# A delta-rule layer feeding a cosine-gated FFN: the first pair's halved inverse widened to full columns in its copy

## The chip, the cores and the metric

The kernel runs on one core of one Trainium2 chip. The metric is the device time of one execution in microseconds (us), taken as the median of several runs. Engines are named as the profile names them: PE (TensorE, matrix products), DVE (VectorE), ACT (ScalarE), POOL (GpSimd) and SP (SyncE, which issues most transfers). "SPq" and "ACTq" are the instructions with which SP and ACT issue a transfer.

## The reference, cut to what matters

There are B = 4 batches, H = 8 heads, S = 768 positions and D = 48 features a head. The first part is a recurrence over the positions; the second is a feed-forward network with 384 inputs and 2048 hidden units, on the 3072 tokens that the recurrence gives.

```python
k_n = k / (norm(k, axis=-1) + 1e-6)
for t in range(S):
    y[:, :, t] = q_t @ state                              # per batch and head
    v_old = state.T @ k_t
    state = state + b_t * outer(k_t, v_t - v_old)
x = y.transpose(0, 2, 1, 3).reshape(B * S, H * D)         # (3072, 384)
h = x @ w_in
out = (h * cos(h)) @ w_out
```

## The kernel before

**Units and pairs.** The recurrence is computed in 24 units of C = 32 positions. Within a unit, the 32 steps are the solution of a lower triangular system, one 32x32 system for each of the 32 pairs of batch and head. Two units make a pair m; the 64 systems of a pair are inverted together, with half of the rows of each inverse in each half of the 128 partitions. The steps of a unit n are: its keys and queries are turned (`turn` on PE, `turn_out` to the tile kq_t on ACT), multiplied (`gram`), scaled and masked on DVE (`gram_keys` gives g, `gram_queries` gives tt), and g is stored to a DRAM scratch tile g_dr (`gram_put`). For a pair, `gram_get` loads g_dr as gb; `invert_eye` sets the inverse z to the identity; `invert` eliminates column after column (the lines 765 and 772); `put` stores z to the scratch tile z_dr; and `get` loads it for each unit in the layout that PE wants. Then `through_state`, `right_side`, `solve`, `solve_out`, `update` and `within` give the unit's outputs and the next state, and `features` and `features_out` turn the outputs into FFN inputs x_ffn.

**The first pair is halved.** All pairs but the first are inverted on POOL, in SBUF. The first pair (m = 0, `HALVED`, units 0 and 1) is inverted on DVE in a PSUM bank, and only as two 16x16 blocks on the diagonal of each system (`fold` brings the two blocks together; HC = 16). Half a of the partitions holds block a. The off-diagonal block g10 is kept in `off_blocks`. Such a unit is then solved in three steps: `solve_half` (p_w), `between` (p_v) and `solve` (p_u), with two copies between them (`half_out` on ACT, `between_out` on DVE, both into the tile u_half). `solve_half` and `solve` use the 32x32 block diagonal of the two inverted blocks, with zeros off the diagonal. In the kernel before this block diagonal lives in `half_zt`, two quarters of the tile halves_z, which is cleared once at the start. `invert_out` copies the 16 by 16 values of a partition from PSUM to SBUF, one `put` stores them, and `get` writes eight pieces a unit into the tile: four batches by two blocks. For unit 0 the four pieces of block 1 are issued by ACT and the others by SP.

**The weights.** w_in and w_out come as 64-bit integers' pairs of words and are put together on three engines, tile by tile: a load (`pairs`), two ACT instructions (532 and 534), two on DVE (538 and 543) and one on POOL (547). Twelve tiles belong to w_in and sixteen to w_out.

**The FFN.** For each pair of units there are hidden products (`hidden`, p_h), the gate h cos h (the lines 1005 to 1024), and output products (p_out). From the second or third pair on they are replaced by schemes with fewer products and more sums (`layer`, `strassen`).

**The order.** The order of all tasks on all engines is written by a list scheduler in Python, `Order`, when the program is built. Each task has an engine, an assumed cost, what it depends on, the buffers it makes and uses, and a due time. `NUDGE` shifts due times, `HOLD` keeps a task back until a time, and `ON_ACT` names the transfers that ACT issues in SP's place. The instructions then stand in that order on each engine and run in order. Every transfer from SP or ACT signals one of eight semaphores, taken in turn in the program's order; before it is issued, the transfer before it on the same semaphore must have landed.

**What sets the order at the start.** PE cannot be kept busy with FFN work until the first units have been through the recurrence and the first weights are there; afterwards the scheduler fills PE with FFN products between the steps of the units.

Of the kernel before, what the change touches and what calls it, by code (L numbers as in the profile page):

```python
# [11 lines left out]
FP = mybir.dt.float32  # L12
# [3 lines left out]
AF = mybir.ActivationFunctionType  # L16

C = 32
DP = 64
SPLIT = 2  # L20
# [25 lines left out]


class Order:
# [9 lines left out]
    WINDOW = 1261.351  # L58
# [14 lines left out]
    EARLY, NUDGE = 6, {('hidden', True): 61.2, ('out', False): 7.4, ('layer', False): 5.9, ('within', False): -4.5, ('hidden', 0, 8): 32.3, ('right', True): -39.1, ('inv', 0, 3): 5.0, ('solve_out', True): -66.4, ('turn', False): 28.3, ('rest', False): 22.3, ('rest', True): -14.8, ('state', False): -8.9, ('layer', True): 9.7, ('solve', True): 4.8, ('left', True): -6.1, ('left', False): 11.8, ('weigh', False): 11.0, ('cos', True): -11.4, ('inv', True): 4.0, ('update', False): -3.7, ('gate', False): 5.6}  # L73


    ON_ACT = {('weights', 9): 1, ('gram_put', 0): 1, ('weights', 14): 1, ('weights', 3): 1, ('gram_get', 1): 1, ('k', 7): 1, ('k', 4): 1, ('q', 3): 1, ('weights', 10): 1, ('gram_get', 2): 1, ('weights', 15): 1, ('weights', 5): 1, ('weights', 17): 1, ('weights', 6): 1, ('put', 0): 1, ('gram_get', 0): 1}
    HOLD = {('v', 5): 82.16, ('k', 8): 77.57, ('add', 9): 86.94, ('norms', 1, 1): 28.35, ('rest', 0, 2): 87.09, ('k', 6): 50.8, ('gate', 0, 4): 90.29, ('split', 11): 68.31, ('shift', 4): 40.04, ('eye', 1): 46.45, ('weights', 14): 75.83, ('features', 1): 93.82, ('split', 8): 56.33, ('split', 10): 65.61, ('get', 2): 96.99, ('half_out', 0): 53.13, ('split', 13): 77.98, ('shift', 5): 40.52, ('gram', 0): 16.72, ('norms', 2, 0): 49.12, ('add', 10): 91.37, ('add', 8): 66.01, ('right', 2): 94.14, ('q', 5): 52.19, ('add', 3): 36.15, ('square', 1, 0): 17.78, ('gram_queries', 2): 46.41, ('shift', 1): 23.89, ('shift', 16): 96.85, ('hidden', 0, 0): 70.69, ('gram_queries', 1): 23.15, ('split', 17): 99.7, ('add', 12): 77.47, ('get', 3): 101.36, ('weigh', 1): 61.19, ('v', 2): 42.92, ('eye', 2): 99.51, ('weights', 2): 18.93, ('gram_put', 2): 29.69, ('hidden', 0, 4): 80.59, ('turn_out', 1): 13.43, ('shift', 9): 60.15, ('weights', 1): 13.99, ('gram_keys', 3): 39.3, ('scale', 0, 0): 13.88, ('square', 3, 0): 65.52, ('turn', 0): 9.1, ('weigh', 0): 44.66, ('scale', 0, 1): 14.96}
# [19 lines left out]
    def add(  # L97
        self, key, engine, cost, emit, deps=(), makes=(), uses=(), moves=0.0, due=1e9
    ):

        assert key not in self.tasks, key
        if key in self.ON_ACT:
            assert moves
            engine = "ACT"
        self.tasks[key] = [engine, cost, due, emit, set(deps), makes, uses, moves]
        for t in uses:
            self.users[t] = self.users.get(t, 0) + 1
        for tag, t in makes:
            self.tiles[t] = tag
# [177 lines left out]
def kernel(  # L287
# [32 lines left out]
    nc = tc.nc  # L320
# [10 lines left out]
    ROWS = C // SPLIT  # L331
# [20 lines left out]
    def half(i):  # L352
        return slice(DP * i, DP * i + DP)
# [13 lines left out]
    def by_parity(t):  # L367
# [33 lines left out]
    def queue(*key):  # L401
        return nc.scalar if key in Order.ON_ACT else nc.sync

# [39 lines left out]
    near = 132 + C  # L443
# [5 lines left out]
    eye = consts[:, 132 + C : 132 + C + ROWS * C].rearrange("p (r i) -> p r i", i=C)  # L449
# [10 lines left out]
    for t in half_tiles:  # L460
        nc.vector.memset(t, 0.0)
        off_blocks.extend((t[:, 0], t[:, 1]))
        half_zt.extend((t[:, 2], t[:, 3]))
# [310 lines left out]
    def invert_out(m):  # L774
        z = work.tile([128, ROWS, C], FP, name="z", bufs=ZS)
        if m < HALVED:
            z = z.rearrange("p r i -> p (r i)")[:, 0 : HC * HC].rearrange(
                "p (r i) -> p r i", i=HC
            )
        nc.scalar.copy(z, zs[m])  # L780
        zs[m] = z

    def put(m):
        width = HC if m < HALVED else C
        z_drs[m] = dram.tile([ROWS, SPLIT, 2, H, B, width], FP, name="z_dr")
        queue("put", m).dma_start(
            out=z_drs[m].rearrange("r s u h b i -> (s u h b) r i"), in_=zs.pop(m)
        )

    def get(n):  # L790

        if n < 2 * HALVED:
            zts[n] = half_zt[n]
            for a in range(2):
                for b in range(B):
                    at = slice(C * b + HC * a, C * b + HC * a + HC)
                    (nc.scalar if a and n == 0 else queue("get", n)).dma_start(
                        out=zts[n][at, :, HC * a : HC * a + HC],
                        in_=z_drs[n // 2][:, a, n % 2, :, b].rearrange("r h i -> r h i"),
                    )  # L800
# [450 lines left out]
    def inverse(m):  # L1251
# [23 lines left out]
        if held:  # L1275
            add(("inv_out", m), "ACT", 0.65, lambda: invert_out(m), deps,
                makes=[("z", ("z", m))], uses=[z])
            deps = [("inv_out", m)]
        add(("put", m), "SP", 0.45, lambda: put(m), deps, makes=[("z_dr", ("z_dr", m))],
            uses=[("z", m)], moves=1.7)  # L1280

    def unit(n):
# [85 lines left out]
        if n < 2 * HALVED:  # L1368
# [11 lines left out]
                [("halves", m), ("u_half", n)] if n < 2 * HALVED else [("zt", n)]  # L1380
            ))
# [269 lines left out]
```

## Time and profile before

| | us |
|---|---|
| three runs | 670.53, 669.92, 669.42 (median 669.92) |
| the profiled execution, its own time | 669.99 |
| its span | 668.2 |
| PE busy in the span | 615.3 (92%) |
| DVE, POOL and ACT busy | 470.1, 348.5 and 246.2 |
| granted TensorE clock | 0.998 |
| packets of the transfers under 512 bytes | 207076 of 215645 |

The profile is of one execution. Its views give the busy time of each engine, the span in equal slices, the groups of instructions by line, and timelines with the time before which an engine was idle and what released it. A releaser is inferred from the semaphores; where a wait is for several of them, the view names the one that came last by its record. PE's instructions of one kind in a row are merged into one line of a timeline. Issue lines (SPq, ACTq) show the time that the issuing takes, not when the data land.

### The profile page before, as it was taken

To read this page: it belongs to the slowest core of one execution; us is meant where nothing else is said; L and a number is where in the kernel's file an instruction comes from. 1 tells how busy PE (TensorE), PEld (TensorE's weight loads), DVE (VectorE), ACT (ScalarE), POOL (GpSimd) and SP (SyncE) were. 2 spreads that over 40 slices of the span, in tenths; PEclk is the share of its full clock that TensorE was granted. 3 is DMA by queue.
4 is the path that set the end of the run, shared out by engine and by line. 5 is a ranking of instruction groups with operands and counts; after the bars stand their busy time and mean duration, and the time that the engine had idled before them with its cause. 6 is when DMAs were issued, how large, how long until landed. Compare 5 with 4: busy or idle time off the path is not lost.

```text
span 668.2 us, 27726 instructions
## 1 busy us (share of the span) xinstructions
PE 615.3 (92%) x12120; PEld 576.3 (86%) x12120; DVE 470.1 (70%) x892; ACT 246.2 (37%) x416; POOL 348.5 (52%) x734
## 2 busy tenths in 40 slices
PE   3316999999999999999999999999999999999997
PEld 3315878887989998999999999989999999989996
DVE  6695679788775875977866867767667656656661
ACT  3433545651243342433434334333324324323420
POOL 4458788978728628458438477158077067000000
PEclk9999999999999999999999999999999999999999
DMA  8866764574455244344434343342311311100000
GB/s 174 205 162 147 180 150 118 135 126 68 73 97 83 51 80 76 53 87 75 64 70 72 67 79 60 63 79 46 71 29 44 50 27 34 25 3 26 1 25 24
DMA packets 215645, 51.80 MB, mean 78 GB/s; under 512 B 207076, under 2 KB 210420, under 8 KB 215524
## 3 DMA queue, kind: packets, MB, share of 16 engines
q1 hardware_dynamic: 204516, 43.39, 34.4%
q10 hardware_dynamic: 10752, 6.20, 3.5%
q8 instruction: 95, 1.56, 1.0%
q0 software_dynamic: 256, 0.44, 0.3%
q14 instruction: 26, 0.21, 0.1%
HBM read 39.24 MB, written 10.75 MB: 75 GB/s over the span
## 4 chain that ended last, share of the span: by engine, by line
PE 82%; POOL 5%; DMA 5%; DVE 4%; issue 2%; ACT 1%; SPq 1%; ACTq 0%; DVEq 0%; POOLq 0%
PE p_h L1084 31%; PE p_out L1167 29%; PE p_kq L822 4%; PE p_h L965 3%; PE p_out L1110 3%; PE p_s L908 2%; PE p_u L885 2%; PE p_kq L925 2%; PE p_g L655 2%; POOL part L765 2%; POOL z L772 2%; PE p_o L1167 2%; PE p_z L944 1%; DMA g_dr<-g 1%; DMA qp<-in_q_dram 1%
## 5 line engine op out<-in xcount | busy, mean ns | idle before, releaser
L765 POOL TENSOR_TENSOR part<-z,gb 128x126 f32<-128x126 f32 (+22 forms) x341 | 135.8, 398 | 134.5 <-DMA gb<-g_dr 77.9
L772 POOL TENSOR_TENSOR z<-z,part 128x126 f32<-128x126 f32 (+22 forms) x341 | 138.5, 406 | 26.7
L1084 PE MATMUL p_h<-x_ffn,w_in 128*128 128x128 f32 x1120 | 145.5, 277 | 1.0 <-issue 1.0
L1084 PEld LDWEIGHTS p_h<-x_ffn,w_in 128*128 128x128 f32 x1120 | 135.5, 192 | 3.7 <-issue 2.1
L1167 PE MATMUL p_out<-w_out,g_ffn 128*128 128x192 f32 x672 | 122.9, 327 | 0.3 <-issue 0.3
L1005 ACT ACTIVATE turns<-p_h,quarter_turn 128x512 int32<-128x512 f32 x96 | 66.0, 687 | 150.3 <-DVE p_h L1103 106.9
L1167 PEld LDWEIGHTS p_out<-w_out,g_ffn 128*128 128x128 f32 x672 | 107.6, 190 | 1.0 <-issue 0.6
L1167 PE MATMUL p_out<-w_sum,g_ffn 128*128 128x192 f32 x496 | 91.3, 329 | 0.0
L1021 ACT ACTIVATE turns<-turns,halfpi 128x512 f32<-128x512 f32 x96 | 69.1, 721 | 42.3 <-DVE turns L1012 40.9
L1012 DVE SCALAR_TENSOR_TENSOR turns<-p_h,turns 128x512 f32<-128x512 f32 x96 | 65.6, 683 | 26.9 <-ACT turns L1005 26.8
L1167 PEld LDWEIGHTS p_out<-w_sum,g_ffn 128*128 128x128 f32 x496 | 79.4, 190 | 1.0
L1183 DVE TENSOR_TENSOR g_ffn<-g_ffn 128x512 f32<-128x512 f32 x88 | 61.9, 704 | 14.8 <-PE p_out L1167 13.9
L1100 ACT COPY g_ffn<-p_h 128x512 f32<-128x512 f32 x60 | 35.2, 586 | 96.4 <-PE p_h L1084 96.1
L1103 DVE TENSOR_TENSOR p_h<-g_ffn,p_h 128x512 f32<-128x512 f32 x60 | 41.7, 695 | 38.6 <-PE p_h L1084 37.8
L1024 DVE TENSOR_TENSOR g_ffn<-turns,p_h 128x512 f32<-128x512 f32 x96 | 64.9, 678 | 5.5 <-POOL w_out L547 3.3
L576 POOL TENSOR_TENSOR knrm<-ksum,halves 128x16 f32<-128x16 f32 (+1 forms) x14 | 37.3, 2665 | 39.8 <-DVE ksum L564 39.8
L965 PE MATMUL p_h<-x_ffn,w_in 128*128 128x128 f32 x384 | 47.7, 283 | 1.5 <-POOL w_in L547 1.3
L965 PEld LDWEIGHTS p_h<-x_ffn,w_in 128*128 128x128 f32 x384 | 45.3, 196 | 2.7 <-POOL w_in L547 1.7
L1217 DVE SCALAR_TENSOR_TENSOR o<-p_out,o 128x192 f32<-128x192 f32 x74 | 25.3, 354 | 29.5 <-PE p_out L1167 29.0
L1084 PE MATMUL p_h<-x_sum,in_sum 128*128 128x128 f32 x320 | 43.1, 278 | 0.7 <-issue 0.7
L1084 PEld LDWEIGHTS p_h<-x_sum,in_sum 128*128 128x128 f32 x320 | 40.2, 191 | 1.4 <-issue 0.8
L624 PE MATMUL p_t<-consts,kp 128*128 128x128 f32 x32 | 7.4, 373 | 31.8 <-DMA halves_z<-z_dr 19.4
(110 smaller groups left out, 780.4 us busy)
## 6 DMA issues: line engine op xcount, KB each, us to landing
pairs<-in_moe_w_out_dram SPq DMA_DIRECT2D x13, 384.0 KB
vp<-in_v_dram SPq DMA_DIRECT2D x96, 48.0 KB
gb<-g_dr SPq DMA_DIRECT2D x18, 256.0 KB
out_dram<-o SPq DMA_DIRECT2D x23, 192.0 KB
pairs<-in_moe_w_in_dram SPq DMA_DIRECT2D x7, 512.0 KB
kp<-in_k_dram SPq DMA_DIRECT2D x128, 24.0 KB
z_dr<-z SPq DMA_DIRECT2D x11, 256.0 KB
zt<-z_dr SPq DMA_DIRECT2D x88, 32.0 KB
```

The costliest lines, as they stand in the source:

```text
L576: nc.gpsimd.tensor_tensor(out=scales[m][2][:, part], in0=sums[m, part.start][:, 0:n], in1=halves[:, 0:n], op=ALU.pow,)
L765: eng.tensor_tensor(out=part, in0=z[:, 0:rows, j, None].to_broadcast(shape), in1=a[:, j, None, j + 1 :].to_broadcast(shape), op=ALU.mult,)
L772: eng.tensor_tensor(out=behind, in0=behind, in1=part, op=ALU.subtract)
L965: nc.tensor.matmul(p_h[:, i], w_in[:, t, (4 * k + i) * 128 : (4 * k + i + 1) * 128], xts[p][:, t, unit * 128 : (unit + 1) * 128], start=(t ...
L1005: nc.scalar.activation(turns[p, f], hidden_of(p, f), AF.Identity, bias=quarter_turn, scale=TURN)
L1012: nc.vector.scalar_tensor_tensor(out=r, in0=hidden_of(p, f), scalar=TURN, in1=t, op0=ALU.mult, op1=ALU.subtract,)
L1021: nc.scalar.activation(r, r, AF.Sin, bias=halfpi, scale=2.0 * math.pi)
L1024: nc.vector.tensor_tensor(out=place(p, f), in0=step_of(rests.pop((p, f)), f), in1=step_of(hidden_of(p, f), f), op=ALU.mult,)
L1084: nc.tensor.matmul(p_h[:, e], in_sum[:, odd_tile, 4 * s + e] if a == "s" else w_in[:, a, f * 128 : (f + 1) * 128], x_sums[p][:, unit] if b ...
L1103: nc.vector.tensor_tensor(out=block(p, s, 0, 1) if i == 3 else p_h, in0=block(p, s, *one), in1=p_h, op=ALU.add,)
L1167: nc.tensor.matmul(p_o, left(p, part, a)[:, e % 4], right(e, b), start=(e == 0), stop=(e == FT // 2 - 1), skip_group_check=True,)
L1183: nc.vector.tensor_tensor(out=left(p, s, to), in0=left(p, s, one), in1=left(p, s, two), op=op)
```

## The change

The copy `invert_out` of the first pair now writes full rows of 32 columns into z: it runs twice, once for each 16 columns, and multiplies by a mask of the partitions (`of_half`, a new constant of two columns), so that a partition of half a gets its 16 values in the columns of block a and zeros in the others. `put` stores z with two transfers, one for each half of the partitions. `get` is then the same as for all the other pairs: four transfers a unit, issued by SP, into a tile zt from a ring of two. `half_zt` is gone and halves_z has half its size. The load of weight tile 6 is no longer issued by ACT. The scheduler's costs of these tasks and its due times, nudges and holds are other values too, so some instructions stand in another order; the order on each engine is the same but for the places that the prediction speaks of and some neighbouring DVE and ACT instructions that change places.

```diff
@@ def _consts():
             p[:, None] // 16 % 2 == np.arange(2)[None, :],
+            p[:, None] // 64 == np.arange(2)[None, :],
             (row[:, :, None] == np.arange(C)).reshape(128, -1),
...
@@ class Order:
-    WINDOW = 1261.351
+    WINDOW = 1329.377
...
-    ON_ACT = {..., ('weights', 17): 1, ('weights', 6): 1, ('put', 0): 1, ('gram_get', 0): 1}
+    ON_ACT = {..., ('weights', 17): 1, ('put', 0): 1, ('gram_get', 0): 1}
...
-        if key[0] in ("k", "gram_put") and key[1] >= 8:
+        if key[0] in ("k", "gram_put") and key[1] >= 8 or key == ("put", 0):
             n //= 2
...
-    off_blocks, half_zt = [], []
+    off_blocks = []
...
-        ffn_pool.tile([128, 4, H, C], FP, name="halves_z", tag="g", bufs=GATES)
+        ffn_pool.tile([128, 2, H, C], FP, name="halves_z", tag="g", bufs=GATES)
...
+    of_half = consts[:, 132 + C : 134 + C]
...
     def invert_out(m):
         z = work.tile([128, ROWS, C], FP, name="z", bufs=ZS)
         if m < HALVED:
-            z = z.rearrange("p r i -> p (r i)")[:, 0 : HC * HC].rearrange(
-                "p (r i) -> p r i", i=HC
-            )
-        nc.scalar.copy(z, zs[m])
+            for a in range(2):
+                nc.scalar.activation(
+                    z[:, :, HC * a : HC * a + HC], zs[m], AF.Copy, scale=of_half[:, a : a + 1]
+                )
+        else:
+            nc.scalar.copy(z, zs[m])
         zs[m] = z

     def put(m):
-        width = HC if m < HALVED else C
-        z_drs[m] = dram.tile([ROWS, SPLIT, 2, H, B, width], FP, name="z_dr")
+        if m < HALVED:
+            z, z_drs[m] = zs.pop(m), dram.tile([2, HC, 2, H, B, C], FP, name="z_dr")
+            for a in range(2):
+                queue("put", m).dma_start(
+                    out=z_drs[m][a].rearrange("r u h b i -> (u h b) r i"), in_=z[half(a)]
+                )
+            return
+        z_drs[m] = dram.tile([ROWS, SPLIT, 2, H, B, C], FP, name="z_dr")
...
     def get(n):
+        zts[n] = work.tile([128, H, C], FP, name="zt")
         if n < 2 * HALVED:
-            zts[n] = half_zt[n]
-            for a in range(2):
-                for b in range(B):
-                    at = slice(C * b + HC * a, C * b + HC * a + HC)
-                    (nc.scalar if a and n == 0 else queue("get", n)).dma_start(
-                        out=zts[n][at, :, HC * a : HC * a + HC],
-                        in_=z_drs[n // 2][:, a, n % 2, :, b].rearrange("r h i -> r h i"),
-                    )
-            return
-        zts[n] = work.tile([128, H, C], FP, name="zt")
-        z_dr = z_drs[n // 2].rearrange("r s u h b i -> u b (r s) h i")[n % 2]
+            z_dr = z_drs[n // 2].rearrange("s r u h b i -> u b (s r) h i")[n % 2]
+        else:
+            z_dr = z_drs[n // 2].rearrange("r s u h b i -> u b (r s) h i")[n % 2]
         for b in range(B):
             queue("get", n).dma_start(out=zts[n][quarter(b)], in_=z_dr[b])
...
-    W_IN, W_OUT, LOADS = -17.551, -72.537, 365.19
+    W_IN, W_OUT, LOADS = -24.522, -78.511, 365.19
...
-    START = 47.26
+    START = 54.45
...
-            add(("inv_out", m), "ACT", 0.65, lambda: invert_out(m), deps,
+            add(("inv_out", m), "ACT", 0.75 if m < HALVED else 0.65, lambda: invert_out(m), deps,
...
-        add(("put", m), "SP", 0.45, lambda: put(m), deps, makes=[("z_dr", ("z_dr", m))],
+        add(("put", m), "SP", 0.98 if m < HALVED else 0.45, lambda: put(m), deps, makes=[("z_dr", ("z_dr", m))],
...
-        add(("get", n), "SP", 1.95 if n == 0 else 3.9 if n < 2 * HALVED else 1.9, lambda: get(n), [("put", m)],
-            makes=[] if n < 2 * HALVED else [("zt", ("zt", n))],
+        add(("get", n), "SP", 1.9, lambda: get(n), [("put", m)],
+            makes=[("zt", ("zt", n))],
```

More of the change, by code (lines that the diff above doesn't have):

```diff
@@ L71 @@
     CHANGE = 0.17
-    EARLY, NUDGE = 6, {('hidden', True): 61.2, ('out', False): 7.4, ('layer', False): 5.9, ('within', False): -4.5, ('hidden', 0, 8): 32.3, ('right', True): -39.1, ('inv', 0, 3): 5.0, ('solve_out', True): -66.4, ('turn', False): 28.3, ('rest', False): 22.3, ('rest', True): -14.8, ('state', False): -8.9, ('layer', True): 9.7, ('solve', True): 4.8, ('left', True): -6.1, ('left', False): 11.8, ('weigh', False): 11.0, ('cos', True): -11.4, ('inv', True): 4.0, ('update', False): -3.7, ('gate', False): 5.6}
@@ L76 @@
-    ON_ACT = {('weights', 9): 1, ('gram_put', 0): 1, ('weights', 14): 1, ('weights', 3): 1, ('gram_get', 1): 1, ('k', 7): 1, ('k', 4): 1, ('q', 3): 1, ('weights', 10): 1, ('gram_get', 2): 1, ('weights', 15): 1, ('weights', 5): 1, ('weights', 17): 1, ('weights', 6): 1, ('put', 0): 1, ('gram_get', 0): 1}
-    HOLD = {('v', 5): 82.16, ('k', 8): 77.57, ('add', 9): 86.94, ('norms', 1, 1): 28.35, ('rest', 0, 2): 87.09, ('k', 6): 50.8, ('gate', 0, 4): 90.29, ('split', 11): 68.31, ('shift', 4): 40.04, ('eye', 1): 46.45, ('weights', 14): 75.83, ('features', 1): 93.82, ('split', 8): 56.33, ('split', 10): 65.61, ('get', 2): 96.99, ('half_out', 0): 53.13, ('split', 13): 77.98, ('shift', 5): 40.52, ('gram', 0): 16.72, ('norms', 2, 0): 49.12, ('add', 10): 91.37, ('add', 8): 66.01, ('right', 2): 94.14, ('q', 5): 52.19, ('add', 3): 36.15, ('square', 1, 0): 17.78, ('gram_queries', 2): 46.41, ('shift', 1): 23.89, ('shift', 16): 96.85, ('hidden', 0, 0): 70.69, ('gram_queries', 1): 23.15, ('split', 17): 99.7, ('add', 12): 77.47, ('get', 3): 101.36, ('weigh', 1): 61.19, ('v', 2): 42.92, ('eye', 2): 99.51, ('weights', 2): 18.93, ('gram_put', 2): 29.69, ('hidden', 0, 4): 80.59, ('turn_out', 1): 13.43, ('shift', 9): 60.15, ('weights', 1): 13.99, ('gram_keys', 3): 39.3, ('scale', 0, 0): 13.88, ('square', 3, 0): 65.52, ('turn', 0): 9.1, ('weigh', 0): 44.66, ('scale', 0, 1): 14.96}
@@ new lines @@
+    EARLY, NUDGE = 6, {('hidden', True): 58.3, ('out', False): 7.4, ('layer', False): 5.9, ('within', False): -4.5, ('hidden', 0, 8): 32.3, ('solve_out', True): -64.9, ('turn', False): 32.4, ('rest', False): 22.3, ('state', False): -8.9, ('layer', True): 9.7, ('solve', True): 4.8, ('left', True): -9.9, ('left', False): 11.8, ('weigh', False): 11.0, ('inv', True): 4.0, ('update', False): -3.7, ('inv', 0, 1): 7.3}
+    ON_ACT = {('weights', 9): 1, ('gram_put', 0): 1, ('weights', 14): 1, ('weights', 3): 1, ('gram_get', 1): 1, ('k', 7): 1, ('k', 4): 1, ('q', 3): 1, ('weights', 10): 1, ('gram_get', 2): 1, ('weights', 15): 1, ('weights', 5): 1, ('weights', 17): 1, ('put', 0): 1, ('gram_get', 0): 1}
@@ new lines @@
+    HOLD = {('v', 5): 82.16, ('k', 8): 77.57, ('add', 9): 86.94, ('norms', 1, 1): 29.51, ('k', 6): 50.8, ('split', 11): 68.31, ('shift', 4): 40.04, ('weights', 14): 75.83, ('features', 1): 93.82, ('split', 8): 56.33, ('split', 10): 65.61, ('get', 2): 96.99, ('half_out', 0): 53.13, ('split', 13): 77.98, ('shift', 5): 40.52, ('gram', 0): 16.72, ('norms', 2, 0): 49.12, ('add', 10): 91.37, ('add', 8): 66.01, ('q', 5): 52.19, ('add', 3): 36.15, ('square', 1, 0): 17.78, ('gram_queries', 2): 46.41, ('shift', 1): 23.89, ('shift', 16): 96.85, ('hidden', 0, 0): 70.69, ('gram_queries', 1): 23.15, ('split', 17): 99.7, ('get', 3): 101.36, ('weigh', 1): 61.19, ('v', 2): 42.92, ('eye', 2): 99.51, ('gram_put', 2): 29.69, ('hidden', 0, 4): 80.59, ('shift', 9): 60.15, ('weights', 1): 13.99, ('gram_keys', 3): 39.3, ('scale', 0, 0): 13.88, ('square', 3, 0): 65.52, ('turn', 0): 9.1, ('weigh', 0): 44.66, ('scale', 0, 1): 14.96, ('turn', 1): 12.38}
@@ L442 @@
     consts = const.tile(list(consts_np.shape), FP, name="consts")
-    near = 132 + C
+    near = 134 + C
     nc.gpsimd.dma_start(out=consts[:, 0:near], in_=consts_dr.ap()[:, 0:near])
@@ L448 @@
     in_half = consts[:, 130 + C : 132 + C]
-    eye = consts[:, 132 + C : 132 + C + ROWS * C].rearrange("p (r i) -> p r i", i=C)
+    of_half = consts[:, 132 + C : 134 + C]
+    eye = consts[:, 134 + C : 134 + C + ROWS * C].rearrange("p (r i) -> p r i", i=C)
     for b in range(B):
@@ L462 @@
         off_blocks.extend((t[:, 0], t[:, 1]))
-        half_zt.extend((t[:, 2], t[:, 3]))
     halves = const.tile([128, 2, H], FP, name="halves")
@@ L1379, in unit @@
             makes=[("two", ("p_u", n))], uses=[("rhs", n) if n else ("vp", m)] + (
-                [("halves", m), ("u_half", n)] if n < 2 * HALVED else [("zt", n)]
-            ))
+                [("halves", m), ("u_half", n)] if n < 2 * HALVED else []
+            ) + [("zt", n)])
         add(("solve_out", n), "DVE", 1.12, lambda: solve_out(n), [("solve", n), scaled],
```

## The prediction

> **What bounds the kernel now.** I read the page's busy strips first, then the chain, then the time by stage, then the instructions of each engine between 40 and 92 us.
>
> ```profile
> span 668.2 us, 27726 instructions
> ...
> PE   3316999999999999999999999999999999999997
> ...
> PE 82%; POOL 5%; DMA 5%; DVE 4%; issue 2%; ACT 1%; SPq 1%; ACTq 0%; DVEq 0%; POOLq 0%
> ```
>
> Each digit of the strip is 16.7 us. TensorE (PE) is idle for most of the first four and full from the fifth on, and 82% of the chain that ended last is PE. So the time is set by when PE becomes full, and by the few holes after that. The stages (columns: stage, its length, busy time of PE, PEld, DVE, ACT, POOL):
>
> ```profile
> 49.30:60.00 10.70, 8.14 (x295) 7.06 (x295) 5.88 (x12) 3.07 (x6) 8.90 (x25) 1.00 0.74 193
> 60.00:67.40 7.40, 3.78 (x191) 3.06 (x189) 4.06 (x8) 2.54 (x5) 6.64 (x12) 1.00 0.54 110
> 67.40:80.00 12.60, 12.59 (x258) 12.11 (x259) 6.98 (x14) 6.40 (x12) 9.59 (x18) 1.00 0.74 184
> 80.00:100.00 20.00, 18.00 (x393) 15.39 (x392) 15.51 (x32) 9.61 (x19) 17.43 (x22) 1.00 0.66 150
> ```
>
> PE is idle 3.6 us in 60 to 67.4, nothing in 67.4 to 80, 2.0 us in 80 to 100. From 100 to 650 it is idle 4.9 us altogether. These are all the holes that an earlier transfer could close. What ends them is in the timelines (start, length, engine, instruction; in brackets the idle time before it and its releaser):
>
> ```profile
> 46.22 1.09 PE L624 MATMUL p_t<-consts,kp 128*128 128x128 f32 x4 [19.36 <-DMA halves_z<-z_dr]
> 49.32 1.81 PE L852 MATMUL p_w<-vp,halves_z 32*32 32x48 f32 x64 [1.16 <-ACT kq_t L634]
> 67.41 1.86 PE L852 MATMUL p_w<-rhs,halves_z 32*32 32x48 f32 x64 [1.32 <-ACT x_ffn L952]
> 91.47 2.72 PE L965 MATMUL p_h<-x_ffn,w_in 128*128 128x128 f32 x22 [1.06 <-POOL w_in L547]
> ...
> 48.68 0.59 ACT L634 COPY kq_t<-p_t 128x512 f32<-128x512 f32 x1
> 65.02 0.84 ACT L559 ACTIVATE ksq<-kp 128x768 f32<-128x768 f32 x1 [4.80 <-DMA qp<-in_q_dram]
> 66.87 0.47 ACT L952 COPY x_ffn<-p_z 128x384 f32<-128x384 f32 x1
> 73.06 0.56 ACT L532 ACTIVATE w_out<-pairs 128x384 f32<-128x384 f32 x1 [1.76 <-DMA pairs<-in_moe_w_out_dram]
> ...
> 45.21 2.45 SPq L797 DMA_DIRECT2D halves_z<-z_dr  x4
> 48.18 4.17 SPq L797 DMA_DIRECT2D halves_z<-z_dr  x8
> 69.13 0.52 SPq L524 DMA_DIRECT2D pairs<-in_moe_w_out_dram  x1
> ...
> 72.08 1.29 POOL L547 TENSOR_TENSOR w_in<-w_in,pairs 128x512 uint32<-128x512 uint32 x1 [1.29 <-DVE w_in L543]
> 78.99 1.01 POOL L547 TENSOR_TENSOR w_out<-w_out,pairs 128x384 uint32<-128x384 uint32 x1 [0.77 <-DVE w_out L543]
> ```
>
> What to see. The first solve (49.32) starts as kq_t's copy ends (48.68 + 0.59 = 49.27): it takes the PSUM bank that turn(4) held. Turn(4) at 46.22 is put down to a transfer of halves_z, which it does not read; in the built program it waits for the DVE's tt(2), which ended at 46.12. The last get of unit 0 on SP ended its issue at 47.66, so the transfer and the copy come due together, and the copy decides. The second solve (67.41) waits for x_ffn's copy, which sat on ACT behind ksq and a split (65.02 to 66.9), and ksq had waited 4.8 us for the last loads of k and q. Those loads stood on SP behind the gets: 2.45 + 4.17 us of issue. The hole at 91.47 waits for POOL, which has worked almost without a gap since 43.7.
>
> **What the skill says.** The Trainium skill, DMA: Bandwidth & Descriptors, Issuing engines are not separate DMA queues: issuing from several engines saves only issue time. Here that issue time is the point: 12 gets cost SP 6.6 us. The same page, Rules for kernel authors, advises against two transfers for two halves of the partitions, since both run over the same engines; the trace of before shows no such pair for the put. VectorE: DVE Perf Modes, The TRN2 errata, gives a ScalarE copy from PSUM as 172 cycles plus one an element at 1.2 GHz: 357 ns for 256 elements, and the trace has 0.37 us for that copy (L780). SBUF — State Buffer, its introduction: a DVE and a POOL instruction can lock each other out of a shared port; agreed, the shift L543 takes 0.42 us alone and 1.50 us beside POOL's adds.
>
> **The change part by part.**
>
> *ACT before the put.* One copy (0.37 us) becomes two of the same size: +0.37 us (between the skill's 0.36 and the 0.62 of a 128x512 copy, should a strided write cost like a full tile; I take 0.37, the row of the same size). One put becomes two issues of 0.38 and a gap of 0.1: +0.45. The put's second half leaves 0.8 us later, 38.6 for 37.8. Behind it on ACT stand a split, ksq and the loads of gb(1), which left at 41.57 after a wait for a g_dr store; ACT had over 1 us to spare there. Four gets leave ACT (2.05 us), which had nothing urgent after them. Cost on the path: 0. The cover is that wait and, for the split, DVE, which takes its result only at 41.5.
>
> *Packets.* 2048 for the put and 1024 a unit for the gets, as before, at 128 bytes for 64. The data is 0.13 MB more each way, in a stretch that moves 300 GB/s: 0.4 us each at most.
>
> *Order on SP.* Every hardware transfer takes one of eight semaphores in turn, and waits for the landing of the one eight earlier. The order of the built program shows what this does. (w0 to w11 are the tiles of w_in, w12 to w27 those of w_out, in the order of loading.) The load of w6 moves from ACT (30.66) to SP (after v at 32.3); it needs 4 us and is used at 38.2, so it costs 0. The load of w7, issued at 38.83 before, must now wait for the first half of the put. The other pairs' full put of 2048 packets took 4.4 us (88.35 to the get at 92.7), so half lands after some 3 us, at 41.2; w7 leaves 2.4 us later. Unit 0's second get waits for w7 (4.4 us, as w11 took from 65.27 to the split at 69.70, so 45.6), the fourth for gb(1) (45.2 before). Gets at 43.9, 45.6, 46.1 and 46.6, the last issued by 47.0 and landed 1.8 later, as k's last load was (63.2 to 65.0): 48.8. The copy at 49.27 still decides. First solve: 0, between 0 and +1 us.
>
> *Further on SP.* The load w8 leaves at 47.1 (47.77), unit 1's four gets at 47.1 to 49.1 in place of 48.18 to 52.35, v to 52. Then q's first transfer waits for the load of w10, issued by ACT at 53.06 and landed by 56.9, when ACT's next transfer on its semaphore went out; so of the 3 us only part survives. Then q, and k for unit 6 at 58.8 to 61 (60.04 to 63.2). SP is 2.2 us ahead; ksq runs at 62.8 and ACT is free when p_z ends at 66.09. x_ffn's copy 0.47, the wait for it 0.07: second solve at 66.65, **0.75 us earlier**. rhs(1) on DVE no longer stands behind the sum either (66.76 before) and is done by 65.9.
>
> *ACT and POOL after that.* The order puts the first w_out split (w12) ahead of u_half(1) on ACT, and w12's add ahead of w11's on POOL. w12 leaves SP at 66.6 in place of 69.13, lands 3.9 later at 70.5, is split by 71.6; u_half is done by 72.1. PE needs it at 66.65 + 1.79 + 4.19 = 72.6: half a microsecond to spare. POOL comes to w12's add at 70.8 and waits for the DVE shift until 72.5 (1.7 for 1.29 us), then has 1.0 + 1.3 us of adds, 3.9 of inverse and 1.0 for w13, whose load is also earlier, so the 0.77 at 78.99 goes: 79.7 for 80.0. If w12 lands 0.7 earlier it is 79.0. So the weights that PE waits for at 91.47 (w9 and w10, behind that inverse on POOL) come 0.3 to 1.0 us earlier. PE arrives 0.75 earlier, so this hole decides: gain **0.3 to 1.0**, and I take 0.7.
>
> *The rest.* halves_z is cleared over 512 columns in place of 1024 (0.91 us before, at 3.9 us, with DVE idle afterwards) and the constants grow by two columns: 0. Unit 0's scale moves within the inverse on DVE, same sum: 0. At two places, one about 205 us, PE, DVE and ACT stand in another order. PE has the same instructions there, and no other engine releases it after 150 us in before: I take 0, and 0.8 either way, out of the 3.8 us of holes from 150 to 650.
>
> Sum: 669.99 (the profiled execution; span 668.2 and 1.8 around it) − 0.7 = 669.3. The median of three runs is 669.92, so 669.2.
>
> **The rivals.**
> *More is won.* If POOL loses both waits, at 72 and 79 (2.06 us), it is ahead by more than PE is, PE's two waits for it near 90 (0.21 + 1.06) close, and the gain is 0.75 + 1.27, with the 0.34 at 111 at most 2.4: 667.5 to 668.5. For it: from 57 us on SP's lead may grow, as four transfers fewer hold its semaphores. Against: w12's add stands ahead of w11's.
> *SP's lead is eaten and the time stays.* The waits for the put, w7 and w10 replace the issue time. ksq then still runs at 65, and PE keeps 67.4: 669.9, within 0.5.
> *Slower: u_half(1) waits behind w12's split.* ACT is in order. If SP is not ahead when it issues w12, the split starts at 73.06 as before, u_half ends at 74.6 and PE, which ran p_v at 73.39, does so 1.2 us later: 671.1. If w7's detour also delays the first solve by 1 us: 672.1. It decides from a landing of w12 after 71.9 on (71.9 + 1.0 + 0.47 = 73.4), microsecond for microsecond. For it: the lead is 2.5 us, made of landings I bounded and did not see. Against: in before SP had idle stretches of 3.3 us at 42 that shrink.
> *The change does not do what it says:* the masks write zeros into the columns that the old tile held as zeros, so solve reads the same values; no more work for PE.
>
> **Numbers.** The forecast (0.3 to 1.0 gained, so 668.9 to 669.6, with the late order 668.1 to 670.4) has a chance of 0.42, the larger gain 0.24, no gain 0.12, the slower case 0.22. A measurement tells about 0.2% here, 1.34 us: 668.6 and 671.3. The forecast gives 0.12 to faster, 0.28 to the same and 0.02 to slower; the larger gain 0.22 and 0.02; the third case is the same; the slower one gives 0.02 to the same. In all 0.34 faster, 0.44 same, 0.22 slower. The range is 667.4 to 671.5: it leaves out the far half of the slower case and the best of the larger gain.
>
> **What would show it.** Right: first solve at 49.3, second at 66.7, ksq by 63, the w12 load issued near 66.6, PE's last wait for POOL at 90.5 to 91.2. Wrong: w7 landing after 46, a first solve that waits for zt, p_v of unit 1 released by u_half, or a PE stage after 100 us with over 1 us more idle than now.

## The result, and the profile after

The changed kernel is slower. Beside the kernel before it took 673.82 us (median of 9 runs) against 671.06 us (9 runs): ratio **1.0042**, 95% interval 1.0026 to 1.0059. A second comparison (after_2 below) gave 1.0067 (1.0041 to 1.0092, 6 runs). The prediction said 669.2 us, range 667.4 to 671.5, and it gave the slower side 0.22. The rival that it called "u_half(1) waits behind w12's split" is what happened; it priced it at 671.1 to 672.1.

One execution of either kernel differs from the next by several us: the runs of the kernel before lie between 667.6 and 677.6. Part of it arises at the start: the fourth run of p_g matmuls on PE (the products of unit 3, ahead of the long first wait) began between 25.5 and 30.0 us in the profiled executions below. Another part arises after PE's last hole for POOL (91 to 99 us), as is shown further down. So times of two profiles are compared here with care: what happened to the whole is read from the medians, and "rest" in the tables is the profiled time less the start of that fourth p_g (before: 669.99 − 25.68 = 644.3; after: 674.50 − 25.52 = 649.0).

The page of the changed kernel, its span, two strips and its chain by engine:

```profile
span 672.7 us, 27716 instructions
...
PE   3316889999999999999999999999999999999997
...
PEclk9999699999999999999999999999999999999999
...
PE 78%; DMA 7%; SPq 4%; POOL 4%; issue 3%; DVE 2%; ACT 1%; ACTq 0%; DVEq 0%; POOLq 0%
```

PE is full from the seventh slice on, where it was full from the fifth: the fifth and sixth slices (67 to 101 us) have 8 for 9. On the chain that ended last, DMA has 7% for 5% and SP's issuing (SPq) 4% for 1%: the added time is upstream of PE. The same four stages as before (stage, length, busy time of PE, PEld, DVE, ACT, POOL, granted TensorE clock, DMA share, GB/s):

```profile
49.30:60.00 10.70, 7.36 (x268) 6.46 (x272) 5.11 (x11) 3.12 (x6) 8.91 (x24) 1.00 0.77 200
60.00:67.40 7.40, 3.75 (x226) 3.13 (x219) 3.42 (x6) 0.95 (x2) 6.69 (x12) 0.82 0.43 73
67.40:80.00 12.60, 9.26 (x162) 8.52 (x161) 5.61 (x10) 5.22 (x11) 5.21 (x9) 0.64 0.77 198
80.00:100.00 20.00, 18.08 (x443) 15.74 (x442) 15.66 (x25) 9.56 (x18) 18.13 (x29) 0.96 0.48 105
```

The loss is in the third: PE is busy 9.26 us of 12.6, where it was busy all 12.59 before, and POOL 5.21 where it had 9.59. Two engines stand still at once. Who holds them is in the timelines of PE, ACT and POOL (start, length, engine, instruction; in brackets the idle time before it and its releaser):

```profile
49.68 1.72 PE L854 MATMUL p_w<-vp,zt 32*32 32x48 f32 x64 [1.16 <-ACT kq_t L635]
...
69.32 1.50 PE L854 MATMUL p_w<-rhs,zt 32*32 32x48 f32 x64 [1.46 <-ACT x_ffn L954]
...
77.58 0.88 PE L854 MATMUL p_v<-u_half,halves_z 32*32 32x48 f32 x64 [1.88 <-ACT u_half L864]
...
96.95 2.72 PE L967 MATMUL p_h<-x_ffn,w_in 128*128 128x128 f32 x22 [1.06 <-POOL w_in L548]
```

```profile
54.24 0.66 ACT L533 ACTIVATE w_in<-pairs 128x512 f32<-128x512 f32 x1 [2.27 <-DMA pairs<-in_moe_w_in_dram]
54.30 0.35 ACTq L525 DMA_DIRECT2D pairs<-in_moe_w_in_dram  x1
...
66.93 0.84 ACT L560 ACTIVATE ksq<-kp 128x768 f32<-128x768 f32 x1 [5.76 <-DMA qp<-in_q_dram]
...
76.19 0.54 ACT L533 ACTIVATE w_out<-pairs 128x384 f32<-128x384 f32 x1 [2.65 <-DMA pairs<-in_moe_w_out_dram]
...
77.06 0.46 ACT L864 COPY u_half<-p_w 128x384 f32<-128x384 f32 x1
```

```profile
78.10 1.01 POOL L548 TENSOR_TENSOR w_out<-w_out,pairs 128x384 uint32<-128x384 uint32 x1 [6.92 <-DVE w_out L544]
```

The first solve is where it was (49.68 for 49.32). The second is 1.9 us later, since ksq starts 1.9 later. Then both late orders bite: w12 is split at 76.19, u_half(1) is copied behind it at 77.06, and p_v, which found its input ready at 73.39 before, waits 1.88 us and starts at 77.58; POOL, with w12's add ahead of w11's, waits 6.92 us, where it waited 1.29 for w11. PE's hole for POOL comes at 96.95 for 91.47.

SP's own timeline and its waits between 38 and 75 us (instruction, what it waited for: total us, times, longest) tell why w12 is late:

```profile
41.66 0.35 SPq L525 DMA_DIRECT2D pairs<-in_moe_w_in_dram  x1
...
59.13 3.06 SPq L420 DMA_DIRECT2D qp<-in_q_dram  x4
62.63 2.53 SPq L420 DMA_DIRECT2D kp<-in_k_dram  x4
...
71.61 1.78 SPq L525 DMA_DIRECT2D pairs<-in_moe_w_out_dram  x1
```

```profile
SPq L420 <- DMA pairs<-in_moe_w_in_dram: 6.0, 2, 3.2
SPq L708 <- DVE g L667: 3.3, 1, 3.3
SPq L525 <- DMA z_dr<-z: 2.5, 1, 2.5
```

SP stood 6.0 us, in two waits, ahead of transfers of q and v until the load of a weight tile had landed; the kernel before has no such wait there. In the built program the two are a transfer of v behind w8 and the first transfer of q behind w10, each sharing a semaphore with it. The 2.5 us are w7's load behind the first half of the put, as predicted.

### The profile page after: what moved, and what is told of

Read it like the earlier page. It is cut to its first block, busy times and chain, and to the rows that moved or that the text cites. A ratio compares the mean times of both kernels' runs of the same rounds, so it can differ in the third digit from the quotient of the medians.

```text
span 672.7 us, 27716 instructions
## 1 busy us (share of the span) xinstructions
PE 616.3 (92%) x12120; PEld 578.1 (86%) x12120; DVE 468.3 (70%) x892; ACT 246.0 (37%) x417; POOL 347.2 (52%) x734
## 4 chain that ended last, share of the span: by engine, by line
PE 78%; DMA 7%; SPq 4%; POOL 4%; issue 3%; DVE 2%; ACT 1%; ACTq 0%; DVEq 0%; POOLq 0%
PE p_h L1086 28%; PE p_out L1169 27%; PE p_h L967 4%; PE p_kq L824 4%; SPq L420 3%; PE p_out L1112 3%; PE p_s L910 2%; PE p_u L887 2%; PE p_kq L927 2%; PE p_g L656 2%; DMA pairs<-in_moe_w_in_dram 2%; PE p_o L1169 2%; SPq L431 2%; POOL part L766 1%; POOL z L773 1%
## 5 line engine op out<-in xcount | busy, mean ns | idle before, releaser
L766 POOL TENSOR_TENSOR part<-z,gb 128x126 f32<-128x126 f32 (+22 forms) x341 | 133.1, 390 | 133.0 <-DMA gb<-g_dr 98.8
L773 POOL TENSOR_TENSOR z<-z,part 128x126 f32<-128x126 f32 (+22 forms) x341 | 140.4, 412 | 26.7
L1086 PEld LDWEIGHTS p_h<-x_ffn,w_in 128*128 128x128 f32 x1120 | 135.4, 192 | 1.5
L967 PEld LDWEIGHTS p_h<-x_ffn,w_in 128*128 128x128 f32 x384 | 47.6, 205 | 2.9 <-POOL w_in L548 1.3
L1219 DVE SCALAR_TENSOR_TENSOR o<-p_out,o 128x192 f32<-128x192 f32 x74 | 25.3, 354 | 28.2 <-PE p_out L1169 27.5
```

Of the source, the lines that this page charges most:

```text
L766: eng.tensor_tensor(out=part, in0=z[:, 0:rows, j, None].to_broadcast(shape), in1=a[:, j, None, j + 1 :].to_broadcast(shape), op=ALU.mult,)
L773: eng.tensor_tensor(out=behind, in0=behind, in1=part, op=ALU.subtract)
L967: nc.tensor.matmul(p_h[:, i], w_in[:, t, (4 * k + i) * 128 : (4 * k + i + 1) * 128], xts[p][:, t, unit * 128 : (unit + 1) * 128], start=(t ...
L1086: nc.tensor.matmul(p_h[:, e], in_sum[:, odd_tile, 4 * s + e] if a == "s" else w_in[:, a, f * 128 : (f + 1) * 128], x_sums[p][:, unit] if b ...
```

## The experiments

A kernel that is said to move a task has the scheduler's plan unchanged; after planning, the named task is moved in the list by which the instructions are written, and nothing else. Such a kernel has six more lines ahead of the copied ones, so L854 of the changed kernel is L860 there. The rivals are: **T1**, the loss is the order of instructions and the semaphores that go with it; **R1**, the loss is the new form itself; **R3**, a lower TensorE clock or a slower fetch of instructions. Ratios are to the kernel before in the same comparison, with their 95% interval.

### Form and order apart

form_alone is the kernel before with the new `invert_out`, `put`, `get`, constant and tiles:

```diff
-    halves_z 4 quarters; one narrow put; get: 8 pieces a unit into half_zt
+    halves_z 2 quarters; two copies with of_half; two puts; get: 4 pieces a unit into zt
     WINDOW, NUDGE, HOLD, ON_ACT, START and the costs: as before
```

> The order of before on every engine, with the new form of the first pair's inverse alone: two copies of the inverse, two puts, four gets a unit. Theory T1 (the loss comes from the new order, and from which transfer has to wait for which because of the eight semaphores, not from the form): the load of w7 waits only for a transfer of v here and leaves near 38.8 us; the second solve starts at 66.7 to 67.5, p_v of unit 1 by 73.5, and the time is that of the kernel before within 1 us (ratio 0.998 to 1.001). Rival R1 (the form costs it: 128-byte packets, two puts, a later copy): most of the 2.8 us is here, ratio 1.003 to 1.005, second solve at 68.5 or later. Rival R3 (a lower TensorE clock or slower instruction fetch in this program): no prediction for the second solve; the stretch from 67 to 80 us would show a clock well under 1.

order_alone is the reverse, the changed kernel's order with the old form:

```diff
     WINDOW, NUDGE, HOLD, ON_ACT, START and the costs: as in the changed kernel
-    two copies with of_half; two puts; get: 4 pieces a unit into zt
+    one copy, one narrow put; get: 8 pieces a unit into half_zt
```

> The form of before (one narrow put, twelve gets) in the new order: the load of w6 on SP, v ahead of q, u_half(1) behind w12's split on ACT, w12's add ahead of w11's on POOL. T1: SP has no lead here, so w12 lands near 72.5 as before, u_half(1) ends near 74.6, p_v of unit 1 starts near 74.6 (before 73.39) and POOL waits 2 to 4 us for w12; ratio 1.002 to 1.005. R1: same as before within 0.1%. If the loss needs both the form and the order (w7 held by the put, which only the two together give), this one shows 1.2 us at most, ratio 1.000 to 1.002.

| kernel | median us (runs) | ratio to before | profiled us | fourth p_g at | rest |
|---|---|---|---|---|---|
| form_alone | 672.30 (22) | 1.0000 (0.9985 to 1.0016) | 672.52 | 28.20 | 644.3 |
| order_alone | 674.59 (22) | 1.0043 (1.0026 to 1.0060) | 676.24 | 27.30 | 648.9 |

The form costs nothing that can be measured (by its interval 0.0016 at most), and the order alone costs as much as the whole change. That is R1 refuted. In PE's timeline of form_alone p_v finds its input ready although the second solve is at 68.38; in order_alone, with the old form, it waits:

```profile
73.49 0.88 PE L854 MATMUL p_v<-u_half,halves_z 32*32 32x48 f32 x64
```

```profile
78.28 0.88 PE L852 MATMUL p_v<-u_half,halves_z 32*32 32x48 f32 x64 [2.43 <-ACT u_half L862]
```

Three details of the expectations were off. The second solve of form_alone was late by 0.9 us against its range, and that cost nothing. In order_alone w12 did not land near 72.5: its split started at 76.89. And there the first solve waited 2.17 us for halves_z, up to 54.08, as SP's gets of unit 0 left at 47.86 (45.21 in before).

**R3**: the clock falls with the same two kernels. Here is the stretch from 67 to 75 us of the changed kernel and of order_alone (columns as above):

```profile
67.00:75.00 8.00, 6.54 (x89) 6.05 (x88) 3.62 (x6) 3.46 (x6) 3.63 (x8) 0.50 0.67 151
```

```profile
67.00:75.00 8.00, 6.56 (x142) 5.95 (x143) 3.50 (x6) 3.56 (x6) 6.01 (x12) 1.00 0.77 181
```

The granted clock is 0.50 in one and 1.00 in the other, with equal loss. form_alone, too, had 0.50 from 65 to 67 us and 0.72 from 67 to 75, without a loss. Instruction fetch had no experiment of its own. What speaks against it: the waits of PE ahead of the second solve that no semaphore explains ("issue", before p_g and p_kq) were 3.66 us in after and 3.69 in a_w12 below, which loses nothing.

### Undoing the late order in the changed kernel

```diff
+    MOVES = [(("half_out", 1), "before", ("split", 12)),   # u_half(1) on ACT: a_act, a_uhalf
+             (("add", 12), "before", ("add", 13))]         # w12's add on POOL: a_pool, a_uhalf
```

Both moves (a_uhalf):

> The changed kernel with two instructions put back in their old places: u_half(1) ahead of w12's split on ACT, and w12's add behind the sixth step of the inverse on POOL. T1: nothing changes until the second solve (69.3), p_v of unit 1 then starts at 75.3 to 75.6 (77.58 in the changed kernel), POOL's 6.9 us wait is under 2, and 1.5 to 2.5 us of the loss come back: ratio 0.999 to 1.001 of before. If the late second solve alone sets the time (T1's other half), only 0.5 us come back, ratio 1.003. R1 and R3: no change, ratio 1.004.

The first alone (a_act):

> The changed kernel with only the ACT half of the earlier repair: u_half(1) goes ahead of w12's split, w12's add stays ahead of w11's on POOL. T2 (both places must be repaired, as PE's hole near 91 to 97 us waits for POOL, and POOL waits 5 to 7 us for w12): p_v of unit 1 no longer waits, but PE then waits 2 to 3 us for POOL at the hole and nothing is gained: ratio to before 1.003 to 1.0045. Rival (PE's wait for u_half is the loss, POOL's is hidden): the ratio falls to 0.998 to 1.001, as with both repairs.

The second alone (a_pool):

> The other half: w12's add goes behind the sixth step of the inverse on POOL, u_half(1) stays behind w12's split on ACT. T2: POOL's wait falls under 2.5 us and its hole no longer decides, so the time is set by PE's own lateness: p_v of unit 1 still waits about 2 us for u_half, of which the 1.1 us hole for POOL takes back half: ratio 1.001 to 1.003. Rival (POOL's wait alone is the loss): 0.998 to 1.001. Rival (u_half alone is the loss): 1.004.

| kernel | median us (22 runs each) | ratio to before | profiled us | fourth p_g at | rest |
|---|---|---|---|---|---|
| a_uhalf | 671.17 | 0.9985 (0.9969 to 1.0000) | 671.60 | 27.03 | 644.6 |
| a_act | 673.49 | 1.0016 (1.0001 to 1.0032) | 673.48 | 28.16 | 645.3 |
| a_pool | 673.31 | 1.0017 (0.9997 to 1.0038) | 675.99 | 29.00 | 647.0 |

Both moves together take back all of the loss, each alone more than half by its median. The expectation for a_act (nothing, since PE would then wait for POOL) was wrong, as was its rival (all). In the traces the two waits are indeed separate. PE's p_v in a_uhalf, and POOL's wait there, now again for w11:

```profile
75.73 0.88 PE L860 MATMUL p_v<-u_half,halves_z 32*32 32x48 f32 x64
```

```profile
74.42 1.29 POOL L554 TENSOR_TENSOR w_in<-w_in,pairs 128x512 uint32<-128x512 uint32 x1 [2.18 <-DVE w_in L550]
```

In a_act POOL still waits 5.21 us (its timeline), in a_pool PE still waits 2.23 (PE's timeline):

```profile
78.07 1.01 POOL L554 TENSOR_TENSOR w_out<-w_out,pairs 128x384 uint32<-128x384 uint32 x1 [5.21 <-DVE w_out L550]
```

```profile
78.04 1.50 PE L860 MATMUL p_v<-u_half,halves_z 32*32 32x48 f32 x64 [2.23 <-ACT u_half L870]
```

### Putting the late order into the kernel before

```diff
+    MOVES = [(("half_out", 1), "after", ("split", 12)),    # b_act, b_late
+             (("add", 12), "before", ("add", 11))]         # b_pool, b_late
```

> The kernel before with only the late order of the changed one: u_half(1) behind w12's split on ACT, w12's add ahead of w11's on POOL; the early part, its transfers and the form stay as they were. T1: w12 is split at 73.06 to 74 as before, u_half(1) ends near 74.5, p_v of unit 1 starts 1.2 us later, POOL waits 3 us more for w12; ratio 1.002 to 1.005. Rival (the late order costs only because w7, w8 and w10 come late in the changed kernel): 1.000 to 1.001.

> The kernel before with only u_half(1) moved behind w12's split on ACT. As the prediction priced it: p_v of unit 1 starts 1.2 us later, and PE's hole for POOL takes some of it back: ratio 1.000 to 1.002. Rival (ACT's half is the mis-sized one): 1.004 or more, with PE waiting over 2 us for u_half.

> The kernel before with only w12's add moved ahead of w11's on POOL. If the price that was left out is POOL's: POOL, which has set PE's last hole in every trace so far, waits 4 to 6 us for w12 in place of 1.3 for w11, less the 1.0 us add and the 0.8 us wait that it no longer has later; ratio 1.003 to 1.005. Rival (POOL's wait is hidden and only both together cost): under 1.001.

| kernel | median us (runs) | ratio to before | profiled us | fourth p_g at | rest |
|---|---|---|---|---|---|
| b_late | 674.95 (6) | 1.0058 (1.0035 to 1.0080) | 676.06 | 27.02 | 649.0 |
| b_act | 674.57 (22) | 1.0033 (1.0015 to 1.0052) | 672.38 | 27.11 | 645.3 |
| b_pool | 673.87 (22) | 1.0020 (1.0001 to 1.0039) | 677.99 | 28.59 | 649.4 |

The two moves alone, with the old form and the old early order, cost as much as the whole change: 0.0058 × 672.2 = 3.9 us. Their parts add within the intervals: 0.0033 + 0.0020 = 0.0053. So the late order as a whole was mis-priced. ACT's half, priced at 1.2 us, cost 0.0033 × 672.4 = 2.2 (by the interval 1.0 to 3.5, so 1.2 is not excluded); POOL's, which the slower rival left out, cost 1.3 (0.1 to 2.6). The expectation that POOL's would be the larger of the two was not borne out, and with these intervals their order is not settled. PE's timelines of b_late and b_act, and POOL's of b_late and b_pool:

```profile
76.88 0.88 PE L858 MATMUL p_v<-u_half,halves_z 32*32 32x48 f32 x64 [1.08 <-ACT u_half L868]
```

```profile
75.39 0.88 PE L858 MATMUL p_v<-u_half,halves_z 32*32 32x48 f32 x64 [1.36 <-ACT u_half L868]
```

```profile
77.41 1.01 POOL L553 TENSOR_TENSOR w_out<-w_out,pairs 128x384 uint32<-128x384 uint32 x1 [6.26 <-DVE w_out L549]
```

```profile
77.27 1.02 POOL L553 TENSOR_TENSOR w_out<-w_out,pairs 128x384 uint32<-128x384 uint32 x1 [5.68 <-DVE w_out L549]
```

Even in the kernel before, w12 comes later than POOL and PE can bear.

### Bringing w12 earlier and keeping the late order

If the late order costs because of when w12 arrives, an earlier w12 must cure it without touching the order. a_w10 moves the load of w10, so that q's first transfer no longer waits for it; a_w12 lets w12's load overtake one group of transfers; a_w6 frees w7 from the put.

```diff
+    MOVES = [(("weights", 10), "after", ("k", 7))]          # a_w10 (and a second profile of it, a_w10_look)
+    MOVES = [(("q", 7), "after", ("weights", 12))]          # a_w12
+    MOVES = [(("weights", 6), "after", ("split", 4))]       # a_w6, with the load issued by ACT as in before
```

> The changed kernel with the load of w10 issued on ACT after the four loads of k for unit 7 in place of before them, so that on SP the first transfer of q no longer has to wait for w10's landing (it shares a semaphore with a transfer of v instead). T1: q leaves at 56 to 57 in place of 59.1, k for unit 6 ends its issue 2 to 3 us earlier, ksq starts at 64 to 65 (66.93), the second solve at 66.6 to 67.5 (69.32), p_v of unit 1 near 74; ratio 0.998 to 1.001. R1: the second solve stays at 69, ratio 1.004. w10 itself lands 2 us later, which may cost PE up to 1 us near 90 in either case.

> The changed kernel with w12's load on SP ahead of the four transfers of q for unit 7, so that it leaves about 1.9 to 2.4 us earlier; the late order and everything ahead of it stay. If the late order costs by w12's arrival, microsecond for microsecond: u_half(1) ends 2 us earlier, p_v of unit 1 waits under 0.5 us, POOL's wait for w12 falls to 4 to 5 us, and 1.5 to 2.4 us come back, ratio 1.000 to 1.002. If the late order costs in itself, whenever w12 comes: 1.004. If the g store or the semaphore before w12 holds it just as long: 1.004, with w12 not leaving earlier in the trace.

> The changed kernel with the load of w6 back on ACT in its old place, which shifts the semaphores so that w7's load waits for a transfer of v and not for the first half of the put. T1 with w7 as the head of the chain (w7 held by the put, so w8 lands late, so w10 leaves late and q behind it): w7 leaves 2 to 2.8 us earlier, w8 lands near 52, w10 leaves near 52.5, q near 57, and most of the loss comes back, ratio 0.999 to 1.002. Rival (w7 is harmless; q's wait for w10's landing is enough by itself): w7 earlier, q still at 58.5 or later after the same start, ratio 1.003 to 1.0045.

> A second profile of the changed kernel with w10's load behind the loads of k for unit 7, since the first profiled execution was the longest of its 23. If the lead on SP brings the gain (T1): counted from the first solve, q leaves at +6 us, ksq starts at +13 to +14, w12 leaves at +18, u_half(1) makes p_v of unit 1 wait under 1 us, and POOL waits 2 to 4 us for w12. If the first profile was typical: ksq at +16, w12 at +21, a wait of 3 us, and the gain in time has another cause.

The column "hole" is the time from w12's leaving to the start of the 22 p_h matmuls that wait for POOL (96.95 in after, 91.47 in before).

| kernel | median us (runs) | ratio to before | profiled us | fourth p_g at | w12 leaves, after that | hole, after that | rest |
|---|---|---|---|---|---|---|---|
| changed kernel | 673.82 (9) | 1.0042 (1.0026 to 1.0059) | 674.50 | 25.52 | 46.1 | 25.3 | 649.0 |
| a_w10 | 671.53 (23) | 0.9984 (0.9967 to 1.0001) | 677.91 | 29.98 | 43.7 | 25.2 | 647.9 |
| a_w10_look | one run, the profiled one | | 671.79 | 28.38 | 41.7 | 24.8 | 643.4 |
| a_w12 | 671.49 (14) | 0.9996 (0.9980 to 1.0012) | 670.68 | 28.22 | 41.5 | 26.1 | 642.5 |
| a_w6 | 673.32 (22) | 1.0020 (1.0003 to 1.0037) | 670.95 | 27.21 | 42.9 | 24.8 | 643.7 |

a_w10 and a_w12 take back all of the loss with the late order still in place. This is the point of the study: **what the late order costs depends on when w12 comes.** In the profiled executions with both late moves, those in which w12 leaves 41.5 to 42.9 us after the fourth p_g have a rest of 642.5 to 643.7; those in which it leaves after 43.7 to 46.1 us (order_alone 44.9 and b_late 43.8 among them) have 647.9 to 649.1. In the rest that looks like a step. Up to PE's hole it is none: in these eight profiles the hole comes 24.8 to 26.1 us after w12 leaves, be it early or late, so there the prediction's "microsecond for microsecond" holds. Without the late order it comes 22.3 to 22.5 us after in before, form_alone and a_uhalf (23.6 and 24.2 in a_both and a_w6ux, where w12 leaves early too): about 3 us is the price of the late order at that place, and an earlier w12 makes up for it. The step comes from what follows the hole, and that differs between single executions (574.9 us in a_w12 to 582.1 in b_pool). One kernel's runs can lie on both sides: the profile of a_w6 is near the lowest of its runs (670.39 to 676.56), that of a_w10 is its highest.

The first profile of a_w10 shows the fault in place (PE waits 3.08 us for u_half); the second shows the mechanism at work. SP's timeline of a_w10_look, POOL's, and ACT's:

```profile
57.30 2.71 SPq L426 DMA_DIRECT2D qp<-in_q_dram  x4
60.45 2.29 SPq L426 DMA_DIRECT2D kp<-in_k_dram  x4
...
70.11 1.52 SPq L531 DMA_DIRECT2D pairs<-in_moe_w_out_dram  x1
```

```profile
76.26 1.01 POOL L554 TENSOR_TENSOR w_out<-w_out,pairs 128x384 uint32<-128x384 uint32 x1 [3.76 <-DVE w_out L550]
```

```profile
75.22 0.46 ACT L870 COPY u_half<-p_w 128x384 f32<-128x384 f32 x1
```

Counted from the fourth p_g, q leaves at 28.9 us (33.6 in the changed kernel), k of unit 6 at 32.1 (37.1), w12 at 41.7 (46.1). u_half(1) ends at 75.68, before PE's p_v at 76.40, which waits for nothing. POOL waits 3.76 in place of 6.92. In a_w12 only w12 moves: PE's timeline has

```profile
76.57 0.88 PE L860 MATMUL p_v<-u_half,halves_z 32*32 32x48 f32 x64 [0.29 <-ACT u_half L870]
```

with the second solve as late as ever (70.81, its first solve at 50.85). So the second solve's 1.9 us of delay are not what is paid for.

a_w6 did half of what was expected. w7 did leave early (12.9 us after the fourth p_g, for 16.1 in the changed kernel), and half the loss came back, but q left 31.4 us after the fourth p_g, no sooner than in a second profile of the changed kernel (31.3). So "w7 as the head of the chain" is wrong for q; what a_w6 gained came with w12, at 42.9 for 46.1 and 44.3, and through which of the steps in between was not settled.

### The changed kernel again, and the best combinations

after_2 is the changed kernel unaltered. a_both has both late moves and a_w10's; a_w6ux has a_w6's in addition.

```diff
+    MOVES = [(("half_out", 1), "before", ("split", 12)), (("add", 12), "before", ("add", 13)),
+             (("weights", 10), "after", ("k", 7))]          # a_both; a_w6ux: and w6's load as in a_w6
```

> The changed kernel itself once more, beside the kernel before on this chip, with more executions. Ratio 1.0035 to 1.005. Its profile gives a second execution: first solve near 50 to 52, second solve 19 to 20 us after it, p_v of unit 1 with a wait of 1.5 to 3 us for u_half, POOL with 5 to 7 us of wait for w12, and 4 to 5 us more than before from the fourth p_g to the end.

> The changed kernel with both repairs of the late order (u_half(1), w12's add) and with w10's load behind the loads of k for unit 7. Each alone gave 0.998 to 0.999. If they repair the same wait from two sides (T1), the second finds nothing left to win: 0.996 to 0.999. If they are independent, the gains add: 4 us under each, 0.992 to 0.994.

> The changed kernel with all repairs: w6's load back on ACT (so that w7 does not wait for the put), w10's load behind k for unit 7 (so that q does not wait for w10), u_half(1) ahead of w12's split and w12's add behind the inverse's sixth step. With the last three alone the ratio was 0.998. If w7's early start adds to it: 0.995 to 0.9975. If POOL, which never rests until the hole, is the floor: 0.9975 to 0.999.

| kernel | median us (runs) | ratio to before | profiled us | fourth p_g at | rest |
|---|---|---|---|---|---|
| after_2 | 676.04 (6) | 1.0067 (1.0041 to 1.0092) | 676.34 | 27.25 | 649.1 |
| a_both | 670.84 (22) | 0.9980 (0.9966 to 0.9993) | 668.86 | 25.63 | 643.2 |
| a_w6ux | 671.72 (14) | 0.9997 (0.9980 to 1.0015) | 671.21 | 27.42 | 643.8 |

after_2 repeats the loss: p_v at 78.24 after a wait of 2.56 us, POOL with 6.75 us for w12. The repairs don't add: a_both is where either repair alone was, as T1 has it, since both take away the same two waits. a_both is 0.2% faster than the kernel before; a_w6ux (0.9997) does not add to it and missed both ranges of its expectation. SP's timeline of a_both, whose fourth p_g stands where before's does, is close to what the prediction had forecast for the change:

```profile
55.26 2.01 SPq L426 DMA_DIRECT2D qp<-in_q_dram  x4
57.70 3.13 SPq L426 DMA_DIRECT2D kp<-in_k_dram  x4
...
67.24 0.51 SPq L531 DMA_DIRECT2D pairs<-in_moe_w_out_dram  x1
```

Forecast were k of unit 6 at 58.8, ksq at 62.8, w12 at 66.6, and 0.7 us won; here it is 57.70, 62.57 and 67.24, and 0.0020 × 672.2 = 1.3 us, but with the late order undone, which the forecast had in place.

## Why the prediction was wrong, step by step

**ACT before the put, and the packets: right.** form_alone prices the whole new form at 1.0000. "w7 leaves 2.4 us later" (41.2) was 41.66; the gets at 43.9 were at 44.46; first solve "0, between 0 and +1": 49.68 for 49.32.

**Further on SP: this step failed.** It had q's first transfer wait for w10, "issued by ACT at 53.06 and landed by 56.9", and concluded that SP is 2.2 us ahead. The semaphore was the right one; the time of w10's landing was mis-sized. w10 left at 54.30 in the profile of after, behind w8's split on ACT, whose load had landed only then; q was released at 59.13, 4.8 us after w10's issue in place of 3.8. In after_2 w10 left on time, at 53.01, and q left at 58.57, 5.6 us later. w10 lands while transfers of k and v run beside it; that they slow it was not tested. q's four transfers then took SP 3.06 us and 0.44 more passed, in place of 1.9 in all. So k of unit 6 left at 62.63, not 58.8: SP was 2.6 us behind before's 60.04, and w12 left at 71.61 in place of 66.6 and took 4.6 us to its split in place of 3.9. a_w10 tests the step: with that one wait taken away the ratio is 0.9984, and the forecast was 0.999.

**Second solve at 66.65: wrong by 2.7 us** (69.32), but a_w12 shows that the time does not hang on it. SP was not the only reason: in a_both ksq ran at 62.57 and the solve still came at 67.83, as p_z ended at 67.26, not at 66.09. The waits of PE just ahead of it that no semaphore explains were 3.66 us there and in after, 2.31 in before; why is open.

**The price of the slower rival: failed too.** It counted u_half(1) on PE, 1.2 us, and not POOL, though the working of the step before it had named w12's add on POOL ahead of w11's, with a wait of 1.7 us; in the profile it was 6.92. On the kernel before, the two moves cost 2.2 and 1.3 us, 3.9 together, where 1.2 had been priced. The point from which it decides, a landing of w12 after 71.9, lay inside the error of a lead "made of landings I bounded and did not see". The chance of 0.22 was too small for it, as w12 in the kernel before already came at 73.06: by its own figures the late order needed the lead, and the lead rested on one bounded landing.

**The hole for POOL decides: right.** PE waits 0.8 to 1.1 us for POOL at that place in every profile but b_act's. It comes 5.5 us later in after, and the profiled time less the start of the 22 matmuls behind it is 578.5 in before, 577.6 in after and 578.7 in after_2: no loss is seen after the hole. **The other order after it, 0 ± 0.8: not contradicted, and not shown so closely**, since that remainder runs from 574.9 to 582.1 over all the profiles that have this hole. **No more work for PE: right**, form_alone takes the same time.

## What to carry to other kernels

When a change comes with a new order, price the order first and on its own: for each instruction that now stands ahead of another on an in-order engine, ask when its input lands and who waits for what is queued behind it, on every engine where the order changed, and add the prices. An estimate that rests on a transfer's landing needs a landing seen in that crowd, not one bounded from a quieter stretch, above all where a shared semaphore puts a whole queue behind it. Weight loads that share a semaphore with inputs of the recurrence are worth moving by a place or two: one such move here won back as much as the whole change had cost.

## What the runs showed that was not expected

- In the two profiles of the changed kernel it took 4.8 and 5.6 us from w10's issue to the release of the transfer on its semaphore. The loads of w12 and w11 in the kernel before took 3.9 and 4.4 us up to their split.
- The start of one execution differs from the next by up to 4.5 us as early as the fourth p_g (25.5 to 30.0 us), and the time after PE's hole near 91 to 99 us by up to 7.2 (574.9 to 582.1).
- SP's issue of one weight load took 0.39 us in some executions and 1.8 in others (w11's, 67.23 with 1.82 us in the profile of after; 67.76 with 0.39 in a_uhalf's).
- The granted TensorE clock was 0.50 from 67 to 75 us in both profiles of the changed kernel and 1.00 in those of order_alone and b_late; the times do not follow it. The Trainium skill (TensorE: Matmul & The Clock Gate, Part 1) says that the clock falls to half after an idle window of about 3.4 us. The traces differ from that: in the profile of after it fell between 64 and 65 us, within a wait of PE of 2.56 us (63.54 to 66.10), with 1.10 us of wait before it at 61. The length of one wait does not decide it either: a_w12 kept 1.00 after a wait of 2.32 us, and a_pool had 0.50 from 78 to 80 us after one of 2.23.
